# Low parts of the first stage by adding DMAs instead of subtractions, in a linear-attention and cosine feed-forward kernel

## The chip, the cores and the metric

One Trainium2 chip, one core of it. The metric is the device time of one execution in microseconds (us), as the median of the runs. The engines are named as in the profile: PE is TensorE (PEld its weight loads), DVE is VectorE, ACT is ScalarE, POOL is GpSimd, SP is SyncE, which issues most DMAs. L12 is line 12 of the kernel.

## The reference

A linear attention with decay runs over 768 steps for 4 batches of 8 heads of 48; its output, 3072 rows of 384, goes through a feed-forward layer of width 2048 with h·cos(h) between the two products.

```python
for t in range(S):                     # B=4, H=8, S=768, D=48
    kt, vt, rt, wt = (k[:, :, t], v[:, :, t], r[:, :, t], w[:, :, t])
    cur = np.einsum('bhd,bhe->bhde', u[None] * kt, vt)
    y[:, :, t] = np.einsum('bhd,bhde->bhe', rt, state + cur)
    state = wt[:, :, :, None] * state + np.einsum('bhd,bhe->bhde', kt, vt)
x = y.transpose(0, 2, 1, 3).reshape(B * S, H * D)
h = x @ w_in                           # 384 -> 2048
g = h * np.cos(h)
out = g @ w_out                        # 2048 -> 384
```

## The kernel before

**Tiling.** The sequence is cut into chunks of 128 steps, 6 in each of 4 batches: 24 chunks, numbered in the order in which they are worked on (two batches alternate). Two chunks make a block of 256 rows. The attention of a chunk has steps with short names: `load` (tile tt, which holds r, k and w transposed), `decay` (two scans, L204 and L211, with r3 and k3 scaled by them, L215 and L216), `diag` (cd and asb), `a` (scores pa, merged into asb at L256), `t` (transposes pt, copied to kn), `d`, `s` (states pst) and `y` (py, copied to yf, and sent by DMAs into xf). `x` turns xf into xT.

**High and low parts.** The products of the feed-forward layer run in fp32r, so every factor is held as a high part (the value cast to fp32r, by `copy`, L133) and a low part (the value less its high part, by `low_part`, L136). A product takes three passes: high by high, high by low, low by high.

**Units.** The feed-forward layer of a block is cut into 8 units of 256 hidden columns. A unit is `mm1` (L363, 18 matmuls into ph), then `gate`, then `mm2` (L377, 12 matmuls into acc). The gate makes g in the tile rr (L340 on ACT, L341 on DVE, L342 and L343 on ACT, L344 on DVE), then its high part into gs (named gh in the tables of engines) and its low part in two halves (g0 and g1). In mm2 the passes are the outer loop, so the first eight of the twelve matmuls read the high part of gs and the last four the low part.

**Weights.** The layer's weights come as 16 blocks of doubles, 768 KB each, by SP (`fetch_weights`) into raw tiles that live in the places of later weights (RING = 5). `load_weights` turns one into fp32: h and rd by ACT (L155, L157), two bit operations and an addition by DVE (L159, L160, L167), then the high part (whi0, ACT, L133) and the low part (wlo0, DVE, L136), each 128 x 2 x 384. The tile h has two buffers, rd has one.

**Order.** Two tables assign operations to engines: EARLY for the first stage, LATER for the rest. The first stage is the list START, which holds the attention of chunks 0 to 5, all 16 weights, and 16 units of blocks 0 and 1, here called t0 to t15. PE's order in it is that of the list; the other engines' order comes from the compiler's scheduler, and each engine then works strictly in its order. From then on the list PLAN repeats, with PE's order by hand. The chunks' loads, xf pieces and the outputs all go through SP's queue, in its order. The tile gs has 2 buffers, tt has 3.

Of the kernel before, what the change touches and what calls it, by code (L numbers as in the profile page):

```python
# [9 lines left out]
F32 = mybir.dt.float32  # L10
# [5 lines left out]
ALU = mybir.AluOpType  # L16
# [14 lines left out]
RING = 5  # L31
BY_HAND = "P"
MERGE = 1
BUFS = dict(tt=3, rk=2, v=4, h=2, rd=1, sign=1, rr=7, gs=2, asb=4, ahl=2, sn=2, yf=1, past=2, xT=2, kn=2, ee=2, dd=2, xf=6, cd=1, rkt=1)
LEAST = 1e-15
W_SCALE = 2.0 ** 8
INV2PI = 1.0 / (2.0 * math.pi)
# [1 line left out]

LAG = 3  # L40
HP = 50
EARLY = dict(rkt="v", cd="a", wsg="v", wadd="v", wm="a", whi0="a", whi1="a", ksh="a", gh="v", yf="a", xh="v", rzh0="p", rzh1="v", r3="v", k3="p", rk="v", ru="p", rf0="v", rf1="v", kn="a", dd="v", rd0="a", rd1="a", rz0="v", rz1="v", ks="v", g0="p", g1="v", x="v", wlo0="v", wlo1="p", qf="s", qt="s", qr="s", qv="s", qx0="s", qx1="s", qo="s")
LATER = dict(ksh="v", gh="v", yf="a", xh="v", rzh0="a", rzh1="a", r3="p", k3="v", rk="v", ru="v", rf0="v", rf1="v", kn="v", dd="p", rz0="v", rz1="v", ks="p", g0="p", g1="p", x="v", qf="s", qt="s", qr="s", qv="s", qx0="s", qx1="s", qo="s")
OFF = 2
FLEAD = 1
LEAD = 0
# [17 lines left out]
def rwkv_cos_ffn(ctx: ExitStack, tc: tile.TileContext, tr, tn, u, ut, wts, w, rkw, vst, us, xs, out):  # L64
    nc = tc.nc
# [23 lines left out]
    def buf(tag, shape, dtype, name=None, pool=sb):  # L89
        return pool.tile(shape, dtype, tag=tag, name=name or tag, bufs=BUFS.get(tag, 1))  # L90
    ident = cst.tile([C, C], F32, name="ident")
# [29 lines left out]
    E = {}  # L121

    def engines(codes):
        E.update({k: {"v": nc.vector, "p": nc.gpsimd, "a": nc.scalar, "s": nc.sync}[e] for k, e in codes.items()})

    def scaled(name, out, in_, by):
        if E[name] is nc.scalar:
            nc.scalar.activation(out, in_, AF.Copy, scale=by)
        else:
            E[name].tensor_scalar(out=out, in0=in_, scalar1=by, scalar2=None, op0=ALU.mult)  # L130

    def copy(name, out, in_):
        (nc.scalar.copy if E[name] is nc.scalar else E[name].tensor_copy)(out=out, in_=in_)  # L133

    def low_part(name, out, full, high):
        E[name].tensor_tensor(out=out, in0=full, in1=high.bitcast(F32), op=ALU.subtract)  # L136

    def fetch_weights(f):
# [6 lines left out]
    def load_weights(f):  # L145

        bits = raw.pop(f)
        wgt[f] = wt.tile([128, 2, 2, DM], F32R, tag=f"w{f}", name=f"w{f}")
        step = 2 if MERGE else 1
        for kind in range(0, 2, step):  # L150
            high, rest = wgt[f][:, kind:kind + step, 0], wgt[f][:, kind:kind + step, 1]
            words = bits[:, kind:kind + step].rearrange("p k (n w) -> p k n w", w=2)
            hi, lo = words[:, :, :, 1], words[:, :, :, 0]
            h = buf("h", [128, step, DM], I32)
            nc.scalar.activation(h.bitcast(F32), hi.bitcast(F32), AF.Copy, scale=2.0 ** -111)  # L155
            rd = buf("rd", [128, step, DM], I32)
            nc.scalar.activation(rd, lo.bitcast(U32), AF.Copy, scale=2.0 ** -29)  # L157
            if E["wsg"] is nc.vector:
                nc.vector.tensor_scalar(out=h, in0=h, scalar1=3, scalar2=None, op0=ALU.logical_shift_left)  # L159
                nc.vector.scalar_tensor_tensor(out=h, in0=hi, scalar=sign_bit, in1=h,  # L160
                                               op0=ALU.bitwise_and, op1=ALU.bitwise_or)
            else:
                sign = buf("sign", [128, step, DM], I32)
                nc.gpsimd.tensor_scalar(out=sign, in0=hi, scalar1=-(1 << 31), scalar2=None, op0=ALU.bitwise_and)
                nc.vector.scalar_tensor_tensor(out=h, in0=h, scalar=three, in1=sign,
                                               op0=ALU.logical_shift_left, op1=ALU.bitwise_or)
            E["wadd"].tensor_tensor(out=h, in0=h, in1=rd, op=ALU.add)  # L167
            hf = h.bitcast(F32)
            copy("whi%d" % kind, high, hf)
            low_part("wlo%d" % kind, rest, hf, high)  # L170
# [149 lines left out]
    def att_x(a):  # L320
        i, ci = divmod(a["j"], BLK)
        if ci == 0:
            xts[i] = buf("xT", [128, 2, KT, BT], F32R)
        xT, cols = xts[i], slice(ci * C, (ci + 1) * C)
        copy("xh", xT[:, 0, :, cols], a["xf"])
        low_part("x", xT[:, 1, :, cols], a["xf"], xT[:, 0, :, cols])
# [9 lines left out]
    def gate(pool, ph):  # L336

        rr = buf("rr", [C, FU, BT], F32, pool=pool)
        nn = rr.bitcast(I32)
        nc.scalar.activation(nn, ph, AF.Copy, scale=INV2PI / W_SCALE)  # L340
        nc.vector.scalar_tensor_tensor(out=rr, in0=nn, scalar=-2.0 * math.pi * W_SCALE, in1=ph, op0=ALU.mult, op1=ALU.add)  # L341
        nc.scalar.activation(rr, rr, AF.Sin, scale=0.5 / W_SCALE)  # L342
        nc.scalar.activation(rr, rr, AF.Square)  # L343
        nc.vector.scalar_tensor_tensor(out=rr, in0=rr, scalar=-0.5, in1=ph, op0=ALU.add, op1=ALU.mult)  # L344
        gs = buf("gs", [C, 2, FU, BT], F32R, pool=pool)
        copy("gh", gs[:, 0], rr)
        for fi in range(FU):
            low_part("g%d" % fi, gs[:, 1, fi], rr[:, fi], gs[:, 0, fi])
        return gs

    def mm1(t):
        i, u = seq[t]
        weights("f", (u + 1) * FU + LEAD + FLEAD)
        weights("w", (u + 1) * FU + LEAD)
        for j in range(BLK):
            att(i * BLK + j, "x")
        xT = xts[i]
        ph = bank("h", [C, FU, BT], "ph")
        for fi in range(FU):
            n = 0  # L360
            for kt in range(KT):
                for a, b in PASSES:
                    nc.tensor.matmul(out=ph[:, fi], lhsT=wgt[u * FU + fi][:, 0, a, kt * 128:(kt + 1) * 128], rhs=xT[:, b, kt],  # L363
                                     start=n == 0, stop=n == 3 * KT - 1)
                    n += 1
        units[t] = gate(sb, ph)
# [27 lines left out]
    for i in PAIR:  # L394
# [8 lines left out]
                 a=att_scores, t=att_transpose, s=att_state, y=att_out, x=att_x)  # L403

    def att(j, n):
        if not 0 <= j < NG or (j, n) in seen:
            return
        for m in ("decay" if n == "diag" and j < BY_PE else NEEDS.get(n, "")).split():
            att(j, m)
        for tag, before in FREES.get(n, ()):  # L410
            for m in before.split():
                att(j - BUFS.get(tag, 1), m)
        if n == "y" and j >= BLK:
            att(j, "s")
        if n == "d":
            att(j - BLK, "s")
        seen.add((j, n))
        if n == "load":
            att_load(j)
        else:  # L420
            steps[n](atts[j])
# [40 lines left out]
    up1 = [0, 0]  # L462
    engines(EARLY)
    with tc.manual_schedule(engines={dict(P=ET.PE, S=ET.SP)[e] for e in BY_HAND}):
        for row in START:
            for e in row.split():
# [4 lines left out]
                else:  # L471
                    att(int(e[-1]), e[:-1])
    engines(LATER)
    with tc.manual_schedule(engines={ET.PE}):
# [24 lines left out]
    with tc.If(some > 0):  # L499
        one_by_one(tc, rkw, vst, us, xs, out, ident, halves, wgt, gate)  # L500
# [137 lines left out]
```

## Time and profile before

| | |
|---|---|
| runs | 578.7, 576.58, 578.22 us; median 578.22 us |
| profiled execution, its own time | 577.43 us |
| its span in the trace | 575.7 us, 11220 instructions |
| mean granted clock of PE | 0.97 |
| DMA | 56.12 MB, mean 97 GB/s |

The slices of the span (40 of equal length, 14.4 us each) show the two stages. Each digit is the busy share in tenths.

```profile
DVE  6999899999997866866957675775676575684431
ACT  2345646654343344334244334333333443343541
POOL 2222134335446445334545444543553443223231
PEclk9976889989999999999999999999999999999998
DMA  8639561013352241142241133133122113420001
```

DVE is full up to slice 12, which is the first stage and its end; ACT and POOL are not. PE's granted clock is below its usual value in slices 3 to 6. The DMA engines are busiest while the weights come in.

### The profile page before, as it was taken

How to read it: one execution, taken by the hardware profiler on the slowest of the kernel's cores; microseconds unless marked ns; L12 is line 12 of the kernel's file. 1: busy time of each engine (PE TensorE's matmuls, PEld its weight loads, DVE VectorE, ACT ScalarE, POOL GpSimd, SP SyncE). 2: the span in 40 equal slices, each digit the busy share in tenths (PEclk: the TensorE clock that was granted, in tenths of full speed). 3: DMA queues.
4: the chain of work that ended last, by engine and by line, in shares of the span. 5: the costliest groups of instructions: out<-in, count | busy, mean ns of one | idle time of the engine just before them, and what ended most of it. 6: DMA issues, size and time to landing. Idle time of an engine off the chain costs nothing.

```text
span 575.7 us, 11220 instructions
## 1 busy us (share of the span) xinstructions
PE 529.5 (92%) x4420; PEld 502.8 (87%) x4420; DVE 424.7 (74%) x732; ACT 240.7 (42%) x398; POOL 227.6 (40%) x272
## 2 busy tenths in 40 slices
PE   1736799989899999999999999999999999999995
PEld 1725689989789999999999999999999999989995
DVE  6999899999997866866957675775676575684431
ACT  2345646654343344334244334333333443343541
POOL 2222134335446445334545444543553443223231
PEclk9976889989999999999999999999999999999998
DMA  8639561013352241142241133133122113420001
GB/s 260 203 127 336 185 227 56 2 55 104 84 177 67 68 131 56 48 132 76 77 131 36 42 111 104 35 97 104 45 88 76 52 40 117 176 95 15 28 1 34
DMA packets 22988, 56.12 MB, mean 97 GB/s; under 512 B 4240, under 2 KB 15120, under 8 KB 22928
## 3 DMA queue, kind: packets, MB, share of 16 engines
q1 hardware_dynamic: 22928, 55.32, 30.7%
q8 instruction: 37, 0.61, 0.5%
q14 instruction: 23, 0.19, 0.1%
HBM read 45.87 MB, written 4.72 MB: 88 GB/s over the span
## 4 chain that ended last, share of the span: by engine, by line
PE 70%; DVE 15%; DMA 7%; issue 3%; ACT 3%; SPq 1%; POOL 0%; DVEq 0%; ACTq 0%; POOLq 0%
PE acc L377 29%; PE ph L363 27%; PE py L306 4%; PE pa L254 4%; DMA tt<-tr 3%; DMA ww<-w 3%; PE py L310 3%; PE pst L281 2%; DVE rr L341 2%; PE pt L263 1%; DVE tt L211 1%; DVE h L167 1%; DVE rr L344 1%; DVE ee L204 1%; DVE h L160 1%
## 5 line engine op out<-in xcount | busy, mean ns | idle before, releaser
L136 POOL TENSOR_TENSOR gs<-rr,gs 128x256 fp32r<-128x256 f32 x176 | 155.6, 903 | 257.7 <-DVE gs L133 194.9
L363 PE MATMUL ph<-xT,w 128*128 128x256 f32 x1728 | 222.5, 285 | 12.9 <-DVE xT L133 9.5
L363 PEld LDWEIGHTS ph<-xT,w 128*128 128x128 f32 x1728 | 215.2, 191 | 16.2 <-DVE xT L133 9.8
L377 PE MATMUL acc<-w,gs 128*128 128x384 f32 x1152 | 220.2, 341 | 1.7 <-DVE gs L133 1.0
L377 PEld LDWEIGHTS acc<-w,gs 128*128 128x128 f32 x1152 | 198.8, 189 | 5.5 <-DVE gs L133 1.3
L342 ACT ACTIVATE rr<-rr 128x512 f32<-128x512 f32 x96 | 60.7, 632 | 137.4 <-DVE rr L341 137.4
L340 ACT ACTIVATE rr<-ph 128x512 int32<-128x512 f32 x96 | 57.1, 594 | 121.8 <-PE ph L363 121.7
L344 DVE SCALAR_TENSOR_TENSOR rr<-rr,ph 128x512 f32<-128x512 f32 x96 | 65.4, 681 | 36.4 <-ACT rr L343 35.5
L341 DVE SCALAR_TENSOR_TENSOR rr<-rr,ph 128x512 f32<-128x512 int32 x96 | 65.2, 679 | 35.4 <-ACT rr L340 35.1
L343 ACT ACTIVATE rr<-rr 128x512 f32<-128x512 f32 x96 | 60.7, 632 | 2.5
L133 DVE CAST gs<-rr 128x512 fp32r<-128x512 f32 x96 | 40.9, 426 | 12.0 <-PE acc L377 12.0
L234 POOL TENSOR_SCALAR_AFFINE_SELECT asb<-cd 128x512 f32<-128x512 f32 x48 | 33.2, 712 | 26.7 <-ACT cd L133 26.6
L204 DVE TENSOR_TENSOR_SCAN ee<-tt,one_e 112x516 f32<-112x516 f32 x24 | 29.8, 1243 | 17.2 <-DMA tt<-tr 17.2
L211 DVE TENSOR_TENSOR_SCAN tt<-tt,inj 112x516 f32<-112x516 f32 x24 | 34.1, 1423 | 0.2
L254 PE MATMUL pa<-tt 48*128 48x128 f32 x384 | 31.8, 298 | 2.3 <-ACT cd L133 2.2
L254 PEld LDWEIGHTS pa<-tt 48*128 48x128 f32 x384 | 26.4, 198 | 8.2 <-issue 3.9
L256 DVE COPY_PREDICATED asb<-mask,pa 128x512 f32<-128x512 uint8 x48 | 32.7, 729 | 1.1 <-POOL asb L234 0.5
L215 POOL TENSOR_TENSOR tt<-tt 112x512 f32<-112x512 f32 x18 | 21.6, 1201 | 27.4 <-DVE tt L211 27.4
L306 PE MATMUL py<-asb,v 128*48 128x128 f32 (+1 forms) x384 | 30.9, 300 | 0.3 <-DVE asb L256 0.3
L306 PEld LDWEIGHTS py<-asb,v 128*64 128x64 f32 (+1 forms) x384 | 24.8, 143 | 1.6 <-issue 0.8
L133 ACT COPY yf<-py 112x512 f32<-112x512 f32 x24 | 13.9, 581 | 20.6 <-PE py L310 20.3
L310 PE MATMUL py<-tt,dd 48*48 48x128 f32 x320 | 22.5, 281 | 0.0
(65 smaller groups left out, 360.6 us busy)
## 6 DMA issues: line engine op xcount, KB each, us to landing
tt<-tr SPq DMA_DIRECT2D x24, 674.2 KB, 5.2
raw<-wts SPq DMA_DIRECT2D x16, 768.0 KB, 7.1
rk<-tn SPq DMA_DIRECT2D x18, 384.0 KB, 3.3
v<-tn SPq DMA_DIRECT2D x24, 192.0 KB, 2.4
out<-ob SPq DMA_DIRECT2D x24, 192.0 KB, 1.9
ww<-w SPq DMA_DIRECT2D x6, 768.0 KB, 4.3
xf<-yf SPq DMA_DIRECT2D x48, 72.0 KB, 3.4
xf<-yf SPq DMA_DIRECT2D x48, 16.0 KB, 2.5
```

Source lines behind the costliest of these rows:

```text
L133: (nc.scalar.copy if E[name] is nc.scalar else E[name].tensor_copy)(out=out, in_=in_)
L136: E[name].tensor_tensor(out=out, in0=full, in1=high.bitcast(F32), op=ALU.subtract)
L211: nc.vector.tensor_tensor_scan(out=wp[:, 0:W129], data0=wp[:, 0:W129], data1=inj.rearrange("p a t -> p (a t)"), initial=0.0, op0=ALU.mult, ...
L254: nc.tensor.matmul(out=pa[h][:, p], lhsT=a["k3"][rows(h), p], rhs=a["r3"][rows(h), p], start=True, stop=True)
L306: nc.tensor.matmul(out=py[ROW * h:ROW * h + m, p], lhsT=a["v"][:, head_cols(p, h)], rhs=a["asb", h][:, p], start=p == 0, stop=not past, sk ...
L340: nc.scalar.activation(nn, ph, AF.Copy, scale=INV2PI / W_SCALE)
L341: nc.vector.scalar_tensor_tensor(out=rr, in0=nn, scalar=-2.0 * math.pi * W_SCALE, in1=ph, op0=ALU.mult, op1=ALU.add)
L342: nc.scalar.activation(rr, rr, AF.Sin, scale=0.5 / W_SCALE)
L343: nc.scalar.activation(rr, rr, AF.Square)
L344: nc.vector.scalar_tensor_tensor(out=rr, in0=rr, scalar=-0.5, in1=ph, op0=ALU.add, op1=ALU.mult)
L363: nc.tensor.matmul(out=ph[:, fi], lhsT=wgt[u * FU + fi][:, 0, a, kt * 128:(kt + 1) * 128], rhs=xT[:, b, kt], start=n == 0, stop=n == 3 * K ...
L377: nc.tensor.matmul(out=accs[i][j][:, :DM], lhsT=gs[:, a, fi, j * C:(j + 1) * C], rhs=wgt[u * FU + fi][:, 1, b], start=u == 0 and fi == 0 a ...
```

## The change

Three operations of the first stage change their engine: the high part of g (gh) goes from DVE to ACT, and the low parts of the weights (wlo0, on DVE before) and of g (g0 on POOL and g1 on DVE before) are made by a DMA that adds. `low_part` takes that way where the table names "s": ACT writes the negated high part to where the low part belongs, and a DMA issued by POOL adds the full value to it there, from SBUF to SBUF. The gate makes the low part of g by one such pair for both halves, so g1 has no use in EARLY. gs gets a third buffer. In LATER only the name "neg" is added, which nothing uses there.

```diff
-BUFS = dict(..., gs=2, ...)
+BUFS = dict(..., gs=3, ...)
...
-EARLY = dict(..., gh="v", ..., g0="p", g1="v", ..., wlo0="v", ...)
+EARLY = dict(neg="a", ..., gh="a", ..., g0="s", g1="v", ..., wlo0="s", ...)
-LATER = dict(ksh="v", ...)
+LATER = dict(neg="a", ksh="v", ...)
...
     def low_part(name, out, full, high):
+        if E[name] is nc.sync:
+            scaled("neg", out, high.bitcast(F32), -1.0)
+            nc.gpsimd.dma_start(out=out, in_=full, accum_op=ALU.add)
+            return
         E[name].tensor_tensor(out=out, in0=full, in1=high.bitcast(F32), op=ALU.subtract)
...
         copy("gh", gs[:, 0], rr)
+        if E["g0"] is nc.sync:
+            low_part("g0", gs[:, 1], rr, gs[:, 0])
+            return gs
         for fi in range(FU):
             low_part("g%d" % fi, gs[:, 1, fi], rr[:, fi], gs[:, 0, fi])
```

After the change the lines behind `low_part` are numbered 4 higher, and those behind the end of `gate` 7 higher. The negation is L128, the adding DMA L138. PE's order is the same in both kernels.

The scheduler places the new instructions, and two places matter. The first is ACT's order around the gate of unit t3 (rr_663 after the change) and the start of that of t4 (rr_740). Here is what stands there after the change; h, rd and w are the tiles of the weights.

```order
L347 ACTIVATE rr_663<-rr_663 128x512
L159 ACTIVATE h_967<-raw_614 128x768
L133 CAST gs_669<-rr_663 128x512
L128 ACTIVATE gs_669<-gs_669 128x512
L133 CAST w10_914<-h_915 128x2x384
L161 ACTIVATE rd_969<-raw_614 128x768
L344 ACTIVATE rr_740<-ph_721 128x512
L128 ACTIVATE w10_914<-w10_914 128x2x384
L133 CAST w11_966<-h_967 128x2x384
L346 ACTIVATE rr_740<-rr_740 128x512
```

In the kernel before, the same place of ACT's order, from the end of t3's gate (rr_655 there) into those of t4 (rr_731) and t5 (rr_773), reads:

```order
L343 ACTIVATE rr_655<-rr_655 128x512
L155 ACTIVATE h_905<-raw_606 128x768
L133 CAST w9_744<-h_745 128x2x384
L157 ACTIVATE rd_907<-raw_606 128x768
L155 ACTIVATE h_956<-raw_608 128x768
L340 ACTIVATE rr_731<-ph_712 128x512
L340 ACTIVATE rr_773<-ph_754 128x512
L342 ACTIVATE rr_731<-rr_731 128x512
```

The weights are ahead by one: where w9 was cast behind t3's gate, w10 and w11 are now. The h of weight w11 (h_967) stands ahead of t3's high part, and takes the buffer that w9's h had, whose last reader is now w9's adding DMA.

The second place is POOL's order from the diagonal tiles of chunk 4 (asb) to the low parts of t4 (gs_746), t5 and t6, after the change:

```order
L220 TENSOR_TENSOR tt_719<-tt_719,ee_795 112x512
L238 AFFINE_SELECT asb_811<-cd_809 128x512
L238 AFFINE_SELECT asb_813<-cd_809 128x512
L138 DMA w11_966<-h_967 128x2x384
L219 TENSOR_TENSOR tt_750<-tt_750 112x512
L138 DMA gs_746<-rr_740 128x512
L138 DMA gs_789<-rr_783 128x512
L138 DMA gs_867<-rr_861 128x512
```

In the kernel before, with the low parts of t3 (gs_661), t4 (gs_737) and t5 (gs_779):

```order
L136 TENSOR_TENSOR gs_661<-rr_655,gs_661 128x256
L234 AFFINE_SELECT asb_801<-cd_799 128x512
L234 AFFINE_SELECT asb_803<-cd_799 128x512
L216 TENSOR_TENSOR tt_710<-tt_710,ee_785 112x512
L136 TENSOR_TENSOR gs_737<-rr_731,gs_737 128x256
L136 TENSOR_TENSOR gs_779<-rr_773,gs_779 128x256
```

The scaled r3 of chunk 6 (tt_750, L219) now stands ahead of t4's low part; before, it came behind all of these. The DMA of weight w11 stands ahead of it too, and a DMA issue waits there for the negation that it adds to.

On SP the loads tt of chunks 4 and 5 now stand together, and the load of chunk 8 stands ahead of the xf pieces of chunk 5, where it stood behind them. On DVE the conversions of weights w12 to w15 stand a few gates earlier than before.

More of the change, by code (lines that the diff above doesn't have):

```diff
@@ L33 @@
 MERGE = 1
-BUFS = dict(tt=3, rk=2, v=4, h=2, rd=1, sign=1, rr=7, gs=2, asb=4, ahl=2, sn=2, yf=1, past=2, xT=2, kn=2, ee=2, dd=2, xf=6, cd=1, rkt=1)
+BUFS = dict(tt=3, rk=2, v=4, h=2, rd=1, sign=1, rr=7, gs=3, asb=4, ahl=2, sn=2, yf=1, past=2, xT=2, kn=2, ee=2, dd=2, xf=6, cd=1, rkt=1)
 LEAST = 1e-15
@@ L41 @@
 HP = 50
-EARLY = dict(rkt="v", cd="a", wsg="v", wadd="v", wm="a", whi0="a", whi1="a", ksh="a", gh="v", yf="a", xh="v", rzh0="p", rzh1="v", r3="v", k3="p", rk="v", ru="p", rf0="v", rf1="v", kn="a", dd="v", rd0="a", rd1="a", rz0="v", rz1="v", ks="v", g0="p", g1="v", x="v", wlo0="v", wlo1="p", qf="s", qt="s", qr="s", qv="s", qx0="s", qx1="s", qo="s")
-LATER = dict(ksh="v", gh="v", yf="a", xh="v", rzh0="a", rzh1="a", r3="p", k3="v", rk="v", ru="v", rf0="v", rf1="v", kn="v", dd="p", rz0="v", rz1="v", ks="p", g0="p", g1="p", x="v", qf="s", qt="s", qr="s", qv="s", qx0="s", qx1="s", qo="s")
+EARLY = dict(neg="a", rkt="v", cd="a", wsg="v", wadd="v", wm="a", whi0="a", whi1="a", ksh="a", gh="a", yf="a", xh="v", rzh0="p", rzh1="v", r3="v", k3="p", rk="v", ru="p", rf0="v", rf1="v", kn="a", dd="v", rd0="a", rd1="a", rz0="v", rz1="v", ks="v", g0="s", g1="v", x="v", wlo0="s", wlo1="p", qf="s", qt="s", qr="s", qv="s", qx0="s", qx1="s", qo="s")
+LATER = dict(neg="a", ksh="v", gh="v", yf="a", xh="v", rzh0="a", rzh1="a", r3="p", k3="v", rk="v", ru="v", rf0="v", rf1="v", kn="v", dd="p", rz0="v", rz1="v", ks="p", g0="p", g1="p", x="v", qf="s", qt="s", qr="s", qv="s", qx0="s", qx1="s", qo="s")
 OFF = 2
```

## The prediction

> **What bounds the kernel now.** I read the page first, then busy time by stretch, then TensorE's waits, then the groups of the first 160 us.
>
> ```profile
> PE 529.5 (92%) x4420; PEld 502.8 (87%) x4420; DVE 424.7 (74%) x732; ACT 240.7 (42%) x398; POOL 227.6 (40%) x272
> ...
> tt<-tr SPq DMA_DIRECT2D x24, 674.2 KB, 5.2
> raw<-wts SPq DMA_DIRECT2D x16, 768.0 KB, 7.1
> rk<-tn SPq DMA_DIRECT2D x18, 384.0 KB, 3.3
> v<-tn SPq DMA_DIRECT2D x24, 192.0 KB, 2.4
> ```
>
> These are the page's busy times and four of its DMA rows (bytes, then us from issue to landing). TensorE is busy for 92% of the span of 575.7 us, so all its idle time is 46 us, and the change can win only out of that. Where it lies, the busy time by stretch says (span, then busy us and count for each engine, granted clock, DMA share, GB/s):
>
> ```profile
> core 0: us, PE busy (x) PEld busy (x) DVE busy (x) ACT busy (x) POOL busy (x), PEclk, DMA share, GB/s
> 0.00:47.00 47.00, 22.23 (x146) 19.61 (x146) 39.73 (x65) 17.80 (x25) 11.27 (x18) 0.89 0.66 212
> 47.00:85.00 38.00, 28.92 (x237) 25.94 (x236) 35.10 (x56) 21.81 (x33) 8.60 (x7) 0.78 0.67 232
> 85.00:125.00 40.00, 37.02 (x279) 35.90 (x279) 40.00 (x64) 24.29 (x39) 15.83 (x11) 1.00 0.15 53
> 125.00:170.00 45.00, 42.86 (x389) 39.93 (x389) 42.12 (x75) 18.48 (x32) 20.14 (x22) 0.96 0.39 113
> 170.00:500.00 330.00, 330.00 (x2879) 314.65 (x2878) 232.92 (x417) 128.89 (x219) 149.11 (x186) 1.00 0.27 79
> ```
>
> From 170 to 500 TensorE has no gap, and the instructions there are those of before. So the change is worth what it moves TensorE by up to about 160, where the first stage ends. There VectorE is full (40.00 of 40 from 85 to 125), but TensorE lacks only 3.0 us in that stretch and 2.1 in the next; its larger gaps are 24.8 us before 47 and 9.1 from 47 to 85. VectorE's fullness is not by itself TensorE's wait. TensorE's waits from 85 to 160, by what ended them (total us, times, longest):
>
> ```profile
> engine line waited for: us in total, times, longest us
> PE pa L254 <- ACT cd L133: 1.6, 1, 1.6
> PE ph L363 <- DVE rr L344: 1.1, 2, 0.9
> PE acc L377 <- DVE gs L133: 1.0, 1, 1.0
> PE ph L363 <- DVE xT L136: 0.7, 1, 0.7
> PE ph L363 <- DVE xT L133: 0.3, 1, 0.3
> ```
>
> **What leaves VectorE and GpSimd.** Line 136 in the first 160 us (shortest/median/longest ns):
>
> ```profile
> L136 DVE TENSOR_TENSOR w<-h,w x16: 932/944/960, 20.7 to 134.2; 128x768 fp32r<-128x768 f32 x16
> L136 POOL TENSOR_TENSOR gs<-rr,gs x16: 732/1418/3345, 54.2 to 153.1; 128x256 fp32r<-128x256 f32 x16
> L136 DVE TENSOR_TENSOR gs<-rr,gs x16: 408/420/974, 54.9 to 153.0; 128x256 fp32r<-128x256 f32 x16
> ```
>
> The same on GpSimd in the rest of the span, and below it the high part of g in the first 160 us, from the groups:
>
> ```profile
> L136 POOL TENSOR_TENSOR gs<-rr,gs x160: 721/739/2180, 168.7 to 566.1; 128x256 fp32r<-128x256 f32 x160
> ```
>
> ```profile
> L133 DVE CAST gs<-rr 128x512 fp32r<-128x512 f32 x16 | 7.1, 444 | 1.3 <-PE acc L377 1.3
> ```
>
> VectorE loses 16 × (0.944 + 0.42 + 0.444), about 29 us. GpSimd loses its 16 subtractions, some 23 us by the median, and keeps 32 issues.
>
> **What ScalarE gets.** Its groups of the first 160 us (busy us, mean ns):
>
> ```profile
> L155 ACT ACTIVATE h<-raw 128x768 f32<-128x768 f32 x16 | 14.5, 907 | 9.8 <-DVE w L136 8.1 <-DMA raw<-wts 1.7
> L157 ACT ACTIVATE rd<-raw 128x768 int32<-128x768 uint32 x16 | 14.5, 905 | 0.0
> L133 ACT CAST w<-h 128x768 fp32r<-128x768 f32 x16 | 13.2, 828 | 11.7 <-DVE h L167 11.7
> L342 ACT ACTIVATE rr<-rr 128x512 f32<-128x512 f32 x16 | 10.1, 631 | 11.9 <-DVE rr L341 11.9
> ```
>
> A negation of a weight has the cast's shape, 0.83; a copy or negation of g that of line 342, 0.6. That is 16 × (0.83 + 0.6 + 0.6), 32.5 us. From 85 to 125 ScalarE has 24.29 of 40. That stretch holds about eight units (279 matmuls less the attention's, 30 to a unit) and five or six weights: 24.3 + 8 × 1.2 + 5 × 0.83 = 38.1 of 40. It goes in order, so the fullness moves there from VectorE.
>
> **The adding transfer** is in no row. From below, 192 KB from memory takes 2.4; from above, 768 KB among the other loads takes 7.1; nothing lets it be free, as the v row shows. For g (262 KB) I take 3.7 with its issue, for a weight (393 KB) 4.5: just over the rk row's 3.3 for 384 KB, with an allowance for GpSimd's issue and for the destination being read too. Both ends stay for the range.
>
> The Trainium skill, "DMA: Bandwidth & Descriptors", section "Anatomy of one DMA — SWDGE (gpsimd) path", fits such a transfer as a fixed 2.0 us plus its bytes over 436e3; that is an estimate of 2.6 us for g and 2.9 for a weight, and by it the time would be that of rival A. No row here shows one yet.
>
> **Where it meets TensorE.** Four places of TensorE, in order of time (start, us, tile, count, idle before):
>
> ```profile
> 42.29 0.58 PE L363 MATMUL ph<-xT,w 128*128 128x256 f32 x1 [9.04 <-DVE xT L133]
> ...
> 52.08 1.01 PE L263 MATMUL pt<-ident,tt 112*128 112x112 f32 x4 [3.78 <-DVE asb L256]
> ...
> 96.07 2.29 PE L377 MATMUL acc<-w,gs 128*128 128x384 f32 x12
> 98.19 2.29 PE L363 MATMUL ph<-xT,w 128*128 128x256 f32 x18
> ...
> 125.15 3.88 PE L363 MATMUL ph<-xT,w 128*128 128x256 f32 x18
> ```
>
> *Up to 53.* The first product ph waits 9.04 for x, whose chunk 1 goes through ScalarE's copy yf, behind a weight's cast. The weights run ahead a little now; I put x at 1.2 earlier (the cast's 0.83 and part of VectorE's 0.944). But behind it
>
> ```profile
> 53.13 0.48 ACT L133 COPY kn<-pt 128x384 f32<-128x384 f32 x1 [1.53 <-PE pt L263]
> ```
>
> kn now finds a negation, a cast and an h ahead of it on ScalarE (0.83 + 0.83 + 0.91 = 2.6 against the 1.5 that it stood idle): the 1.2 are given back. Sum at 53: **0**.
>
> *53 to 85.* The attention's own chain (scores, transposes, states) is as before, and the copies on ScalarE that it needs get negations ahead of them: between 0 and one of 0.83. I take **+0.5** at 85.
>
> *Unit t4* (the fifth; its acc starts at 96.07). Of a unit's 12 products acc the last four read the low part: 96.07 + 8/12 × 2.29 = 97.6. Before, it is there at 97.3:
>
> ```profile
> 93.64 1.84 DVE L211 TENSOR_TENSOR_SCAN tt<-tt,inj 112x516 f32<-112x516 f32 x1
> 95.41 0.40 DVE L133 CAST gs<-rr 128x512 fp32r<-128x512 f32 x1
> ```
>
> GpSimd's part of the same unit, and below it its group of r3 in the first 160 us:
>
> ```profile
> 95.95 1.39 POOL L136 TENSOR_TENSOR gs<-rr,gs 128x256 fp32r<-128x256 f32 x1 [1.56 <-DVE gs L133]
> ```
>
> ```profile
> L215 POOL TENSOR_TENSOR tt<-tt 112x512 f32<-112x512 f32 x2 | 2.6, 1304 | 4.5 <-DVE tt L211 4.5
> ```
>
> The low part is there 1.9 us after the high part's start, with 0.3 us in hand. After the change the same piece is a cast, a negation and the transfer: 0.6 + 0.6 + 3.7 = 4.9, so 3.0 more. The start of it moves as well. VectorE's scan no longer stands in the way (−1.7). But h of weight w11 stands on ScalarE ahead of t3's cast and waits for w9's adding transfer, since h has two buffers: 4.5 less the 0.91 + 0.63 + 0.91 + 0.63 = 3.1 that ScalarE has to do meanwhile, **+1.4**. Then r3 of chunk 6 (1304 ns) stands on GpSimd ahead of t4's transfer: half of it, +0.7. With the +0.5 at 85 the start goes from 95.4 to 96.3 and the landing to 101.2; the products want it at 98.1. TensorE stands for 3.1: unit t4 ends **3.6 later** than before, the 0.5 included. The units behind are one product apart from it and shifted with it, so I count no second stall.
>
> *After t4.* TensorE is now late by 3.6, and what it waited for comes from an eased VectorE: of the five waits above, all but the 0.7 (which lies ahead of t4) go, 4.0 us. The 18 products ph at 125.15 took 3.88 where others take 2.29; 1.6 more may go. From the 5.6 I take **−4.5**, since ScalarE's cd (the 1.6) now has more ahead of it.
>
> *Third gs buffer.* It takes away the 1.3 us that VectorE waited for acc; VectorE no longer does that cast. It costs nothing and gains nothing on its own.
>
> *SP's order.* The load tt of chunk 8 goes ahead of chunk 5's xf pieces. At best 0, as the DMA share there is 0.39; at worst the xf pieces wait for a load of 5.2 (its row). I take 0, since the load's buffer comes free with the same chunk that feeds xf; if that cover goes, it is up to +5.2 once.
>
> **Sum.** +3.6 − 4.5 = **−0.9** against the profiled execution's own 577.43 (span 575.7 and 1.7 around it): 576.5. The median of the three runs, 578.22, is 0.8 above that execution, so **577** for the median.
>
> **The rivals.**
>
> *A, faster: the stall at t4 isn't there.* If transfers land 1.3 to 1.5 us sooner (as the 192 KB row's 2.4 suggests), both h's wait and the low part gain, 2.8 together, and the stall falls from 3.1 to 0.3: 577.43 + 0.5 + 0.3 − 4.5 = 573.7, by the median 574.5. If the freed VectorE also shortens the wait of 3.78 at 52 (it is for VectorE's asb), it is 571 to 574. For it: VectorE is full wherever TensorE waits. Against it: TensorE's clock and its gaps before 85 belong to the attention's chain, not to weights.
>
> *B, slower: ScalarE becomes the bound, through h.* Each us that a transfer is later counts twice at t4 (h of the weight after next, then g's own). It decides from 2 us more than I took, 5.7 for g: then the sum is −0.9 + 4.0 = +3.1, 581.3 by the median. At 7.1 (the raw row) it is 3.4 + 2.6 = 6.0 more: 582.5, by the median 583; a second unit caught in the same way adds the weight's 2.6: 586. For it: 38.1 of 40 on an engine that goes in order. Against it: the DMA share from 85 to 125 is 0.15, so the queues are empty there.
>
> *D, slower: GpSimd's issue is held up while VectorE works.* GpSimd's subtraction took 1418 ns in the median where VectorE was full and 739 later, 3345 at the longest, so the two disturb each other. If an issue takes what the longest lost, 3.345 − 0.739 = 2.6, both transfers on t4's path come 2.6 late, +5.2: 581.7, by the median 582.5. By the medians' difference of 0.7 it is only +1.4. VectorE is also less full now.
>
> The Trainium skill, "SBUF — State Buffer", section "SBUF: two separate sides", states a rule against this change: a transfer issued by GpSimd can't get its descriptors written while VectorE holds the shared port in a two-port mode. The rows of line 136 agree that the two engines hold each other up; that descriptors do, no run shows yet.
>
> *C: it changes nothing on TensorE's path.* The relief isn't where TensorE waits and the new latency is covered by the units' distance: 578.2. Against it: only 0.3 us was in hand at t4.
>
> **How the numbers follow.** Forecast 0.34, A 0.26, B 0.20, D 0.12, C 0.08. The range takes in A's and B's ends, with half of chunk 8's load on top: 570.5 to 589. About 0.5% (2.9 us, 575.3 to 581.1) is what a measurement can tell from no change. A and the low edge of the forecast give faster 0.29; B, D and the forecast's upper edge slower 0.34; the rest, 0.37, is the same.
>
> **What would show it.** The adding transfers' rows: 3.7 for g, 4.5 for a weight (2.4 is A, over 5.7 B or D). TensorE's acc of unit t4 should wait for gs by about 3 us near 98, once, and the waits for cd and rr after 105 should be gone. ScalarE should be at 38 of 40 from 85 to 125 with h waiting for a DMA. VectorE should have lost about 29 us before 160. From 170 to 500 TensorE should stay without a gap; a gap there would make all of this wrong, as would a first ph that is more than 1.2 us away from 42.3.

## The result, and the profile after

| | before | changed |
|---|---|---|
| median | 578.46 us | 617.45 us |
| ratio | 1 | 1.0676, 95% interval 1.0647 to 1.0705 |
| span of the profiled execution | 575.7 us | 613.7 us |

The change makes the kernel 39 us slower; the prediction, 577 with a range up to 589, was wrong. Busy time by stretch of the changed kernel, with the columns of the prediction:

```profile
0.00:47.00 47.00, 19.04 (x129) 16.27 (x129) 36.25 (x57) 17.96 (x26) 15.22 (x21) 1.00 0.75 203
47.00:85.00 38.00, 23.18 (x187) 20.85 (x189) 22.49 (x34) 22.18 (x34) 10.24 (x9) 0.68 0.81 235
85.00:125.00 40.00, 26.37 (x140) 24.27 (x137) 26.20 (x40) 20.08 (x32) 11.61 (x11) 0.71 0.69 177
125.00:170.00 45.00, 40.13 (x317) 37.58 (x316) 27.06 (x41) 35.12 (x58) 15.71 (x18) 1.00 0.64 124
170.00:210.00 40.00, 34.57 (x307) 31.99 (x306) 24.62 (x47) 16.28 (x29) 12.03 (x16) 0.96 0.57 148
210.00:540.00 330.00, 329.45 (x2869) 313.62 (x2866) 241.02 (x413) 128.91 (x219) 147.20 (x186) 1.00 0.27 79
```

From 210 on TensorE is as full as it was from 170, so nearly all is lost before. From 85 to 125 it ran 140 products instead of 279, and no engine is busy in its place: VectorE 26.2 of 40 where it was 40.0, ScalarE 20.1. If one of them were short of time it would be full there; here all of them wait. The DMA share went from 0.15 to 0.69: half of it (0.33) is SP's transfers, 4.56 MB in that stretch for 2.06 before, since loads now run there that were through by then; the other half (0.35) is the adding transfers themselves.

TensorE's busy time, from the page of the changed kernel, has grown too, for the same 4420 products (529.5 us before):

```profile
PE 539.2 (88%) x4420; PEld 509.7 (83%) x4420; DVE 411.6 (67%) x684; ACT 268.4 (44%) x446; POOL 232.4 (38%) x288
```

So of the 38 us by which the span is longer, 28 are TensorE standing, and 10 are products that took longer. The granted clock was 0.68 from 47 to 85 and 0.71 from 85 to 125, where it was 0.78 and 1.00. No run takes this clock apart from the waits; in the run without transfers below, where h doesn't wait for any, it was 0.82 and 0.96.

ScalarE's longest waits in the first 210 us, then VectorE's, then TensorE's (us in total, times, longest):

```profile
ACT h L159 <- DMA w<-h: 33.6, 7, 10.0
ACT cd L133 <- PE pc L226: 11.4, 4, 6.2
```

```profile
DVE h L163 <- ACT h L159: 30.4, 7, 8.5
DVE rr L348 <- ACT rr L347: 9.0, 7, 2.1
```

```profile
PE ph L370 <- DVE xT L133: 16.8, 2, 10.4
PE pc L226 <- DVE rkt L205: 15.0, 3, 6.4
PE acc L384 <- DMA gs<-rr: 12.2, 6, 4.0
PE pt L267 <- DVE asb L260: 11.0, 2, 10.3
```

The waits for xT, rkt and asb stood in the kernel before as well, up to 170:

```profile
PE pc L222 <- DVE rkt L201: 13.1, 3, 6.2
PE ph L363 <- DVE xT L133: 9.5, 3, 9.0
PE pt L263 <- DVE asb L256: 4.9, 2, 3.8
```

So what is new is mainly 7.3 us for xT, 6.1 for asb, and 12.2 for g's low part (gs). The first two are one chain, read upwards through the three blocks of the changed kernel. TensorE waits for attention tiles of VectorE, which has time enough, but stands at a weight's h, which ScalarE hasn't written, as it waits for a weight's adding transfer to let go of the buffer. Three of ScalarE's seven waits for it are long (9.7, 10.0 and 8.3). The first long one, on GpSimd (with the transfer's time to landing), ScalarE and VectorE (start, us, idle before):

```profile
42.99 1.27 POOL L138 DMA_DIRECT2D w<-h  x1 [4.03 <-ACT w L128]
...
DMA to landing us min/median/max: 10.2/10.2/10.2
```

```profile
42.57 0.89 ACT L159 ACTIVATE h<-raw 128x768 f32<-128x768 f32 x1
53.19 0.89 ACT L159 ACTIVATE h<-raw 128x768 f32<-128x768 f32 x1 [9.73 <-DMA w<-h]
```

```profile
54.11 0.56 DVE L163 TENSOR_SCALAR h<-h 128x768 int32<-128x768 int32 x1 [7.12 <-ACT h L159]
54.59 0.68 DVE L205 TENSOR_TENSOR rkt<-tt 112x512 f32<-112x512 f32 x1
55.19 1.23 DVE L208 TENSOR_TENSOR_SCAN ee<-tt,one_e 112x516 f32<-112x516 f32 x1
```

The transfer landed at 42.99 + 10.2 = 53.2, and the next h started there. Behind the h on VectorE stand rkt and the scan of a chunk, on which the scores, the transposes and the next x hang. So a late weight, for which TensorE wasn't waiting, stopped the attention. ScalarE's next long wait of h, until 91.56, held up its copy yf (94.28), and behind it the pieces of xf and the next x. On TensorE the two arrive as:

```profile
62.07 1.01 PE L267 MATMUL pt<-ident,tt 112*128 112x112 f32 x4 [10.30 <-DVE asb L260]
...
105.03 0.58 PE L370 MATMUL ph<-xT,w 128*128 128x256 f32 x1 [6.39 <-DVE xT L133]
```

The waits for gs hang on it in part: two of the six, 3.7 of the 12.2 us, are for transfers that went out at 94.00 and 114.65, right behind ScalarE's second and third long wait of h (until 91.56 and 112.27), since g's cast and negation stand behind h there.

The transfers themselves (issue on GpSimd, shortest/median/longest ns, and from issue to landing in us; weights first, then g):

```profile
L138 POOL DMA_DIRECT2D w<-h x16: 1193/1212/1409, 20.7 to 160.0; - x16
...
DMA to landing us min/median/max: 4.2/4.8/12.3
```

```profile
L138 POOL DMA_DIRECT2D gs<-rr x16: 849/890/916, 67.1 to 186.2; - x16
...
DMA to landing us min/median/max: 3.2/4.1/11.2
```

The medians are near what the prediction took (4.5 and 3.7). The longest are not: 12.3 and 11.2, and the long ones make the long waits. What SP had issued when the 12.3 us transfer of 79.2 was under way:

```profile
74.15 1.15 SPq L147 DMA_DIRECT2D raw<-wts  x2
75.40 1.53 SPq L185 DMA_DIRECT2D tt<-tr  x2
82.37 0.35 SPq L147 DMA_DIRECT2D raw<-wts  x1
```

That is 3 × 768 and 2 × 674 KB on the core's 16 DMA engines. The Trainium skill, "DMA: Bandwidth & Descriptors", section "Queues, rings and completion order", says that each engine takes turns between the queues that have work, a packet at a time. The trace agrees in that the transfer didn't go ahead of the loads: it landed at 91.5, and the last of these loads, issued 3.2 us after it, within half a microsecond of that. The two other weights' transfers of over 10 us, issued at 42.99 and 101.51, had loads beside them as well.

### The profile page after: what moved, and what is told of

Its sections match the earlier page's. It is cut to its first block, busy times and chain, and to the rows that moved or that the text cites. A ratio compares the mean times of both kernels' runs of the same rounds, so it can differ in the third digit from the quotient of the medians.

```text
span 613.7 us, 11333 instructions
## 1 busy us (share of the span) xinstructions
PE 539.2 (88%) x4420; PEld 509.7 (83%) x4420; DVE 411.6 (67%) x684; ACT 268.4 (44%) x446; POOL 232.4 (38%) x288
## 3 DMA queue, kind: packets, MB, share of 16 engines
q0 software_dynamic: 6656, 10.49, 9.9%
## 4 chain that ended last, share of the span: by engine, by line
PE 62%; DMA 6%; DVE 4%; issue 1%; POOL 1%; ACT 0%; DVEq 0%; POOLq 0%; SPq 0%
PE ph L370 26%; PE acc L384 26%; DMA tt<-tr 4%; PE pa L258 3%; PE py L310 3%; PE py L314 2%; DMA gs<-rr 2%; PE pst L285 1%; PE pt L267 1%; POOL gs L140 1%; DVE tt L215 1%; DVE rr L348 1%; DVE ee L208 1%; DVE rr L345 1%; DVE xT L140 1%
## 5 line engine op out<-in xcount | busy, mean ns | idle before, releaser
L370 PE MATMUL ph<-xT,w 128*128 128x256 f32 x1728 | 227.6, 289 | 22.8 <-DVE xT L133 16.8
L370 PEld LDWEIGHTS ph<-xT,w 128*128 128x128 f32 x1728 | 219.9, 195 | 27.2 <-DVE xT L133 17.5
L384 PE MATMUL acc<-w,gs 128*128 128x384 f32 x1152 | 223.9, 344 | 12.2 <-DMA gs<-rr 12.2
L140 POOL TENSOR_TENSOR gs<-rr,gs 128x256 fp32r<-128x256 f32 x160 | 125.3, 803 | 193.8 <-DVE gs L133 179.2
L219 POOL TENSOR_TENSOR tt<-tt 112x512 f32<-112x512 f32 x18 | 23.4, 1300 | 46.2 <-DVE tt L215 41.3
L138 POOL DMA_DIRECT2D w<-h x16 | 19.9, 1241 | 39.2 <-ACT w L128 13.5
L138 POOL DMA_DIRECT2D gs<-rr x16 | 14.2, 884 | 53.7 <-ACT gs L128 42.6
L159 ACT ACTIVATE h<-raw 128x768 f32<-128x768 f32 x16 | 14.3, 895 | 38.2 <-DMA w<-h 33.6
L215 DVE TENSOR_TENSOR_SCAN tt<-tt,inj 112x516 f32<-112x516 f32 x24 | 30.7, 1277 | 0.3
```

Source lines behind the costliest of these rows:

```text
L215: nc.vector.tensor_tensor_scan(out=wp[:, 0:W129], data0=wp[:, 0:W129], data1=inj.rearrange("p a t -> p (a t)"), initial=0.0, op0=ALU.mult, ...
L384: nc.tensor.matmul(out=accs[i][j][:, :DM], lhsT=gs[:, a, fi, j * C:(j + 1) * C], rhs=wgt[u * FU + fi][:, 1, b], start=u == 0 and fi == 0 a ...
```

## The experiments

Each ratio is to the kernel before, run on the same chip.

**Weights alone.** The gate as before, two gs buffers:

```diff
-gs=3 ... gh="a" ... g0="s"
+gs=2 ... gh="v" ... g0="p"
```

> Only the weights' low parts go by negation and adding DMA; the gate is that of before (high part on VectorE, low halves on GpSimd and VectorE, two gs buffers). Theory H (held buffer): a weight's adding transfer queues with the loads on the DMA engines, takes up to 12 us, holds one of the two h buffers, and ScalarE, which goes in order, stands at the next h. Then most of the loss is here: 600 to 615 us, with h waiting some 30 us for the transfer. Theory S (ScalarE's work, 32.5 us more of it): only 13 of the 32.5 us are here, 585 to 595, and no wait of h matters. Theory G (latency of the gate's low part): 570 to 580, as before or a little faster.

Measured 611.49 us, ratio 1.0561 (1.0523 to 1.0599). Most of the loss is here, as theory H said, and ScalarE's longest wait is that of the changed kernel:

```profile
ACT h L159 <- DMA w<-h: 35.7, 10, 9.9
```

**Gates alone.**

```diff
-wlo0="s"
+wlo0="v"
```

> Only the gates' part: high part of g, negation on ScalarE and adding DMA, three gs buffers; the weights' low parts stay a subtraction on VectorE. Theory H: little loss, 575 to 585, since nothing holds h. Theory S: 19 of the 32.5 us of work are here, 595 to 605. Theory G: most of the loss, 600 to 615, with acc waiting 10 us or more for the gates' transfers.

584.91 us, ratio 1.0103 (1.0063 to 1.0143). So theory G falls. The gates' part alone costs some 7 us, and acc waits 6.8 us for gs in it; and with 19 of the 32.5 us of ScalarE's new work in it, it lost far less than theory S said.

**No transfers.**

```diff
         scaled("neg", out, high.bitcast(F32), -1.0)
-        nc.gpsimd.dma_start(out=out, in_=full, accum_op=ALU.add)
         return
```

> The changed kernel without the adding DMAs: ScalarE casts and negates as there, VectorE and GpSimd are as eased, and the low parts hold the negated high part (so the output is not the reference's). Theories H and G: the transfers are the loss, so 565 to 580. Theory S: the loss stays, 605 to 617, since ScalarE's work is unchanged.

574.86 us, ratio 0.9942 (0.9912 to 0.9972). With all of ScalarE's new work the kernel is 3.4 us faster than before; ScalarE is then at 34.35 of 40 from 85 to 125:

```profile
85.00:125.00 40.00, 35.65 (x252) 34.51 (x250) 30.61 (x48) 34.35 (x57) 5.54 (x4) 0.96 0.22 81
```

So theory S falls: ScalarE's work is not the bound, and the loss goes with the transfers. It also says what the change is worth without them: VectorE and GpSimd eased, by about 29 us on VectorE, and ScalarE's work added give 3.4 us net.

**Three buffers of h.**

```diff
-h=2
+h=3
```

> The changed kernel with three buffers of h instead of two. Theory H: a transfer of 10 us now holds one of three, and h waits for the transfer of three weights ago: the wait of h falls from 33.6 to under 15 us and the time to 585 to 603. Theories S and G: 612 to 618, no change.

605.31 us, ratio 1.0450 (1.0412 to 1.0488): 12 us back, less than the theory said, and h still waits 26.5 us. ScalarE's negation and GpSimd's rows show something new:

```profile
45.26 0.84 ACT L128 ACTIVATE w<-w 128x768 fp32r<-128x768 f32 x1
```

```profile
49.68 1.20 POOL L138 DMA_DIRECT2D w<-h  x1 [7.35 <-DVE inj L214]
60.68 1.21 POOL L138 DMA_DIRECT2D w<-h  x1 [9.80 <-issue]
```

The second issue had its data: the negation ahead of it ended at 46.1. GpSimd stood for 9.8 us with no releaser, up to the landing of the first transfer (49.68 + 10.7 = 60.4). So two weights' transfers are not under way at once, even with a buffer free. In the changed kernel too, no weight's transfer was issued before the last one had landed.

**Without the loads.** One raw block for all 16 conversions, in the kernel before and in the changed one:

```diff
+    if f > 0:
+        raw[f] = raw0[0]
+        return
```

> The kernel before with one block of raw weights loaded once and used for all 16 conversions (15 loads of 768 KB left out, so the output is not the reference's). It is the base for the next run; 560 to 580 by every theory, since its DMA wait for raw tiles is 1.7 us in all.

577.48 us, ratio 0.9956 (0.9936 to 0.9976), the base for the next run.

> The changed kernel with the same 15 loads left out. Theory HQ (the transfer is long because it shares the DMA engines with bursts of loads, and so holds h): the longest landing of a weight's transfer falls from 12.3 to under 7 us, h waits for it under 12 us in all instead of 33.6, and the time is at most 12 us over the same kernel of before without the loads. Theory HL (even an undisturbed transfer of 4 to 5 us is too long for two buffers of h on an engine that goes in order): the waits stay above 20 us and the difference above 20 us.

593.27 us, ratio 1.0250 (1.0211 to 1.0289): 15.8 us over its base instead of 39. The answer lies between the two theories. Without these loads a weight's transfer takes 8.3 at most, h waits 14.4 us, no wait over 3.7; some 60% of the loss needs the loads, the rest doesn't.

```profile
ACT h L163 <- DMA w<-h: 14.4, 8, 3.7
```

**Copies instead of additions.**

```diff
-nc.gpsimd.dma_start(out=out, in_=full, accum_op=ALU.add)
+nc.gpsimd.dma_start(out=out, in_=full)
```

> The changed kernel with plain copies instead of adding transfers: the same bytes are read from SBUF and written to it, nothing is added (so the low parts hold the full value, and the output is not the reference's). If the addition, with its second read, is what makes a transfer long, the median landing of a weight's transfer falls from 4.8 to about 3.5 us and the time to 590 to 605. If queueing and the fixed part are, landing and time stay, 612 to 618.

599.68 us, ratio 1.0345 (1.0319 to 1.0371). Somewhat under half of the loss goes with the addition. Issue and landing of a weight's copy:

```profile
L138 POOL DMA_DIRECT2D w<-h x16: 698/728/1050, 21.2 to 146.6; - x16
...
DMA to landing us min/median/max: 2.8/3.2/9.5
```

An addition costs 1.6 us more in the median than a copy (4.8 to 3.2), and GpSimd's issue 1212 ns instead of 728. All 32 transfers together took 29.0% of the DMA engines' time in the first 210 us as additions, and 17.4% as copies of the same bytes.

**Four buffers of h**, two of gs:

```diff
-h=2 ... gs=3
+h=4 ... gs=2
```

> The changed kernel with four buffers of h, and two of gs to make room. With three buffers 605.3 us were measured and h still waited 26.5 us. If the hold of h is what is left, four bring 590 to 600 and a wait under 15 us. If the conversions are bound by the transfer's end in another way (the negation's issue on GpSimd, in order behind other work), it stays at 603 to 608.

606.40 us, ratio 1.0455 (1.0423 to 1.0487): no better than three, though what the lost buffer of gs costs is not taken apart here. GpSimd's waits without a releaser are now the largest that it has:

```profile
POOL w L138 <- issue: 27.8, 5, 8.3
```

**A larger descriptor ring** (the space for the descriptors of GpSimd's transfers, a parameter of the kernel), first in the changed kernel, in which nothing else differs, then with four buffers:

```diff
-dynamic_dma_scratch_size=1024
+dynamic_dma_scratch_size=4096
```

> The changed kernel, instruction for instruction, with 4096 instead of 1024 bytes for the descriptors that GpSimd writes. Theory R (ring): 1024 bytes hold one weight's adding transfer but not two, so GpSimd stands at the second issue until the first has landed, and all behind it too; in the run with three buffers of h GpSimd stood 9.8 and 8.1 us with no releaser shown, up to a landing. Then two weights' transfers overlap here and the time falls to 600 to 612. Theory HQ (the hold of h by a queued transfer alone): with two buffers of h a second issue hardly ever comes before the first has landed, so nothing changes, 614 to 619.

612.78 us, ratio 1.0565 (1.0506 to 1.0623), against 1.0676 (1.0647 to 1.0705): about 6 us back, between what the two theories said. The ring is a part of the loss, and a small one while two buffers of h come first.

> Four buffers of h, two of gs, and 4096 bytes for descriptors; with 1024 bytes it was 606.4. Theory R: GpSimd's unexplained waits ahead of issues (27.8 us) go, h waits under 8 us, 588 to 598. Theory HQ without the ring: 603 to 608 as before.

600.74 us, ratio 1.0348 (1.0284 to 1.0411). GpSimd's unexplained waits are gone, but only 6 us with them, fewer than theory R said, and h still waits 11.1 us. Now two weights' transfers run side by side with the loads and take 6.8 in the median and 17.0 at the longest, and the gates' transfers among them:

```profile
PE acc L384 <- DMA gs<-rr: 20.2, 4, 10.4
```

**Without any adding DMA: g's high part on ScalarE, three gs buffers**, in the kernel before:

```diff
-gs=2 ... gh="v" ... wlo0="v"
+gs=3 ... gh="a" ... wlo0="v"
```

> The kernel before with only the high part of g on ScalarE and three buffers of gs; no adding DMA. VectorE loses 7.1 us, ScalarE gets 9.6. If VectorE's work is worth little on TensorE's path, as the run without the transfers showed (574.9 with 29 us less on VectorE), it gives 574 to 578.

580.80 us, ratio 1.0020 (0.9994 to 1.0047): no change, a little above what was expected. Then also the weights' low parts on GpSimd:

```diff
-wlo0="v"
+wlo0="p"
```

> As the last, and the weights' low parts subtracted on GpSimd instead of VectorE (15.1 us less on VectorE, some 30 more on GpSimd, in the same two buffers of h). If h being held longer is harmful by itself, also without a DMA, it is slower than the last by 3 to 10 us; if only a transfer holds it long enough, 572 to 577.

597.00 us, ratio 1.0286 (1.0227 to 1.0344): 16 us slower than the last, more than the 3 to 10 expected. It is the same kind of wait without a DMA. A subtraction on GpSimd takes 1849 ns instead of VectorE's 944, waits in GpSimd's order, and ScalarE's next h waits for it twice as long as it did for VectorE's in the kernel before (8.1 us). How much of the 16 us this is, beside weights that are ready later, is not shown.

```profile
ACT h L155 <- POOL w L136: 16.5, 9, 2.9
```

**The transfer doesn't hold h.** The weights' transfers read a tile of zeros instead of h; the second kernel has 3072 bytes of ring as well:

```diff
-nc.gpsimd.dma_start(out=out, in_=full, accum_op=ALU.add)
+nc.gpsimd.dma_start(out=out, in_=full if name == "g0" else still, accum_op=ALU.add)
```

> The changed kernel in which the weights' adding transfers read a tile of zeros that nothing writes, instead of h (so the low parts hold the negated high part, and the output is not the reference's). The bytes, the addition, GpSimd's issues and the loads beside them are as in the changed kernel; only h is no longer held by the transfer. Theory H (the hold of h): the waits of h for transfers are gone and the time is 576 to 590, near the run with the gates' part alone (584.9). Theory T (the transfers' traffic on the DMA engines and GpSimd's issues slow everything): 603 to 617.

600.46 us, ratio 1.0387 (1.0352 to 1.0421): 17 us back with the traffic as it was, between the two theories: the hold is real, but it is not all. ScalarE no longer waits for transfers; GpSimd does, at issues with no releaser, with the gates' transfers behind it in its order. TensorE's longest wait, then GpSimd's:

```profile
PE acc L386 <- DMA gs<-rr: 17.8, 6, 10.3
```

```profile
POOL w L140 <- issue: 16.1, 4, 7.8
```

> As the last, with 3072 bytes for the descriptors. If the ring alone is what is left when h is not held, 3 to 10 us less than the last; if not, the same within 3 us.

588.84 us, ratio 1.0188 (1.0154 to 1.0222): another 12 us, a little more than expected. GpSimd's waits at these issues are gone. The largest wait of TensorE that the kernel before doesn't have is now for g's low part:

```profile
PE acc L386 <- DMA gs<-rr: 10.8, 6, 4.8
```

Read as steps from the changed kernel, in shares of the time before: 1.0676, less 2.9% for the hold of h, less 2.0% for the ring, less 2.5% for what the transfers do besides, gives 0.9942 without them. Each step holds the slower products in it as well as the waits. The order matters: the ring is worth 1.1% while h is held and 2.0% once it isn't. The scheduler orders ScalarE and VectorE a little differently in some of these kernels, so the shares aren't exact; PE's order is fixed by hand.

## Why the prediction was wrong

**What failed** is the step at unit t4: "4.5 less the 0.91 + 0.63 + 0.91 + 0.63 = 3.1 that ScalarE has to do meanwhile, **+1.4**". It names the right mechanism, h waiting for the adding transfer of the weight two before, and prices it once, at one place, by a typical transfer. It happened seven times for 33.6 us, and three of the waits were 8.3 to 10.0. At the very place, the h of weight w11 ahead of t3's cast, 8.31 stood for the 1.4, as w9's transfer took 10.7 us to land instead of 4.5:

```profile
112.27 0.90 ACT L159 ACTIVATE h<-raw 128x768 f32<-128x768 f32 x1 [8.31 <-DMA w<-h]
113.07 0.60 ACT L133 CAST gs<-rr 128x512 fp32r<-128x512 f32 x1
```

Two things were missed in it. The transfer's length was taken as a figure of its own, while it was 4.8 in the median and 10.2 to 12.3 beside loads that SP had just issued: the weights' conversions run exactly while the weights come in. And the wait was charged to the weight and its unit alone, not to what stands behind h on ScalarE and VectorE in their orders, which is the attention's chain.

**Rival B** had this mechanism, and its price was too low for the same reason: its end of 7.1 us, the median of the raw row, is no upper bound for a transfer beside a burst of such loads; 12.3 was measured. Its counterargument, a DMA share of 0.15 from 85 to 125, was read from the kernel before; there the share became 0.69, with loads that had come late and with the transfers themselves. It also looked at one stretch only: the first long transfer began at 42.99, where the prediction's own table has 0.66 and 0.67.

**Up to 53, "0", and 53 to 85, "+0.5"**: the loss began there, ahead of t4. The first ph started 3.4 late (45.71 for 42.29), more than the 1.2 that the prediction named as a sign of being wrong, and the transposes of 52.08 came at 62.07, 10.0 late. The prediction looked for h's wait only behind t3.

**Unit t4, "3.1" of waiting for the low part**: right in kind, acc did wait for gs, but for 1.67 us at t4, about half. And it recurs, in six waits of up to 4.0, so "I count no second stall" was wrong; the kernel with the gates' part alone is 6.7 us slower than before.

```profile
129.07 0.96 PE L384 MATMUL acc<-w,gs 128*128 128x384 f32 x4 [1.67 <-DMA gs<-rr]
```

**ScalarE "38.1 of 40"**: it was 20.08, as it stood for transfers; without them 34.35. That the sum gave this fullness no price of its own was right.

**"−4.5" after t4**: in the changed kernel nothing was won back. TensorE was 29.8 late at t4's first acc (125.84 for 96.07) and is 38.0 late at the end; between lie three more waits for gs, 6.9 us. That easing VectorE is worth a few us is borne out only by the run without the transfers, 3.4 us net of ScalarE's added work.

**Rival D**, GpSimd's issue held up by VectorE, didn't happen in the size that it needs. The issues took 1193 to 1409 ns and 849 to 916. The rule of the Trainium skill that stands beside it ("SBUF — State Buffer", "SBUF: two separate sides") names such a stall, and the changed kernel shows at most a trace of it: the four longest weight issues, 1267 to 1409 ns, ran beside VectorE's first operation on an h (L163), and the other twelve took 1193 to 1233. GpSimd's issue was held up by the ring instead, which none of the prediction's cases had.

**The fit of the Trainium skill** ("DMA: Bandwidth & Descriptors", "Anatomy of one DMA — SWDGE (gpsimd) path"), 2.6 and 2.9 us: plain copies landed in 2.5 and 3.2 in the median, which is near; the adding ones took 4.1 and 4.8.

**Rival C** held for two parts of the change: a third gs buffer and ScalarE's cast of g together changed nothing (1.0020).

**"SP's order", taken as 0**, is not settled: VectorE waited 12.1 us for tt loads in the first 210 us, where it was 5.1 up to 170 before. In the run without the transfers it waited 9.7, and that kernel is not slower than before, which speaks against a large share.

What stays open is how the last 2.5% divide between the traffic of the transfers and the latency of g's low part, what lowers TensorE's clock while it waits more, and how many bytes of the ring an adding transfer takes. No whole version here beats the kernel before: the two that are faster leave out the additions or the loads.

## What to carry to other kernels

In these runs a transfer that replaced an instruction held its source until it landed, so first count the buffers of its source and name what stands, on each engine in order, behind the next writer of that buffer. Price it at every place where it recurs, and by its longest case beside the loads of that stage, not by a typical row. And relief of a full engine is worth only what the bound engine waits for: here 29 us less on VectorE, with ScalarE's added work, gave 3.4 without the transfers.

## What the runs showed of the hardware

- An adding SBUF-to-SBUF transfer of 393 KB landed in 4.8 us in the median and a copy of the same bytes in 3.2; GpSimd's issue took 1212 and 728 ns. The 32 adding transfers took 29.0% of the 16 DMA engines' time in 210 us, the copies of the same 10.49 MB 17.4%.
- Beside loads that SP had just issued, weights' adding transfers took 10.2, 10.7 and 12.3 us to land.
- With 1024 bytes of descriptor space GpSimd stood at an issue until the weight's transfer before it had landed (9.8 us once), with nothing in the profile as releaser but "issue"; with 3072 or 4096 bytes these waits were gone, and the time fell by 2.0% in the kernel whose transfers don't hold h.
- The same 4420 products kept TensorE busy for 529.5 us before and 539.2 us after; the granted clock from 47 to 125 was 0.78 and 1.00 before, 0.68 and 0.71 after.
